# Clustered attention with a routed expert layer: row maxima three steps further ahead, results scaled one head later

## The chip, the cores and the metric

The kernel runs on one core of one Trainium2 chip. A core has five engines that run side by side, each with its own instruction stream: TensorE (PE, matmuls into PSUM; its weight loads are listed as PEld), VectorE (DVE), ScalarE (ACT), GpSimd (POOL) and SyncE (SP, which here only issues DMAs). They wait for each other by semaphores. The metric is the device time of one execution in microseconds (us); lower is better.

## The reference

Two layers are computed. The first is attention for 2 batches x 8 heads, 768 positions, head size 64, in which a query sees only the keys of its own cluster:

```
q_assign = argmax(q_n @ c_n)          # 16 centroids per head
k_assign = argmax(k_n @ c_n)
scores = scale * q @ k.T, or -1e9 where the two assignments differ
attn = softmax(scores);  attn_out = attn @ v
```

The second takes the 1536 tokens (512 numbers each), sends every token to the expert with the largest gate logit (8 experts, at most 384 tokens each), and computes `gate * (relu(x @ w1[e]) @ w2[e])`.

## The kernel before

**Heads and groups.** The 16 (batch, head) pairs are worked off one after the other by a loop over `i`; a head has 12 groups `g` (written below as 6:8, head 6, group 8). Each group issues, in `st_group`, two matmuls of 384 columns for one tile of transposed scores (`s`, L395 and L396; float32 work is done as products of high and low parts) and an exponential on ACT (`pf`, L400). Beside them stands one tile of the row maxima for a later head: `max_tile` issues one matmul (`m`, L335) and one DVE reduction (`mx`, L342). The `m` tiles have two PSUM banks, the `s` tiles three. So in most groups PE issues three matmuls, DVE makes one reduction and ACT one exponential.

**What hangs on the groups** is placed by `hooks(i, g)`, called after each group:

- g = 2 (`G_B1`) and g = 8 (`G_B0`): the two halves of `pv_batch`, 12 matmuls with v into the bank `o` (pool `psO`, one bank). At g = 2 the head before is finished: `p_add` on DVE (`acc`, L406), then `sum_strips` on PE (`rsp`, L432), which sums the exponentials and whose second half reads `acc`; ACT empties both banks (`rs` L443, `oT` L425). At g = 8 stands the `p_add` of the current head's first half.
- g = 5: `sum_turn` (PE transposes `rtp`, L450) and `max_chain`; g = 6: `sum_scale` (DVE, `r`, L456 to L458).
- g = 7: `max_rows` transposes the next head's maxima (`mtp`, L373), ACT copies them (`mr`, L375), SP sends them into row `Qs` of the next head's operand; then `out_stage` (`otp`, L522) turns the result of the head before. `rtp`, `mtp`, `otp` and the cluster tiles `ctb`, `ccp`, `ctp` share the two banks of pool `psT`.
- g = 8: `out_scale` on DVE (`lt`, `lg`, `x`: L543 to L545).
- Even heads assign clusters for the pair of heads two pairs ahead: scores at g = 2, `cl_turn` at g = 4 (`ctp`), the first DVE steps of `cl_assign` at g = 8 (`cmx`, `ceq`), a product on POOL, and the last two (`cm`, `ohb`) at g = 2 of the next head.
- `split` prepares the operands of head i+3: ACT copies at g = 2 and g = 8, each followed by three GpSimd subtractions (`ql`, `Y`, L298) and SP transfers.
- The gate of the first batch (`gate(0)`) begins at 8:9: small DVE steps, matmuls `gps` on PE, and at its end six indirect DMAs on GpSimd that scatter the tokens into the array `xd`. A load of 128 rows of `xd` (`row0`) is issued on SP at 9:6.
- Four `w_split` of expert weights (ACT copy L131, DVE subtraction L137) stand at 12:10, 13:10, 14:4 and 14:10 (`W_AT`).

PE, DVE and ACT keep the written order from head 1 on (`keep`). After the heads, `moe` runs the experts, nearly all of it on PE.

Of the kernel before, what the change touches and what calls it, by code (L numbers as in the profile page):

```python
# [23 lines left out]
def kernel(  # L24
# [655 lines left out]
    def hooks(i, g):  # L680
# [3 lines left out]
        if (i, g) == (H, G_B0 + 1):  # L684
            gens["g"] = gate(0)
        if i == H and g > G_B0 or i == H + 1 and g < 2:
            next(gens["g"], None)
# [3 lines left out]
        if (i, g) in W_AT:  # L691
            c = W_AT.index((i, g))
            w_split(c)
            w_load(c + NA)
# [9 lines left out]
        if g == G_CHAIN and i + 1 < NH:  # L704
            max_chain(i + 1)
        if g == G_ROWS and i + 1 < NH:
            max_rows(i + 1)
        if (i, g) == (H + 1, 4):
# [463 lines left out]
    with ExitStack():  # L1172
        for i in range(NH):
# [3 lines left out]
            for g in range(2 * NT):  # L1177
                st_group(i, g)
                if i == 0 and g < NT:
                    max_tile(1, g, 0, warm=WARM1)  # L1180
                    max_tile(1, g, 1)
                else:
                    n, k = (i + 1, NT + g) if g < NT else (i + 2, g - NT)
                    if n < NH:
                        max_tile(n, k // 2, k % 2)
# [85 lines left out]
```

## Time and profile before

| | us |
|---|---|
| median of 3 runs | 489.12 (489.0 to 489.14) |
| the profiled execution | 489.03 |
| its span from first to last instruction | 486.9 |
| PE busy in it | 449.3 (92%) |
| DVE busy | 319.9 (66%) |
| ACT busy | 273.9 (56%) |
| POOL busy | 128.2 (26%) |
| one reduction `mx` (L342), mean of 192 | 0.552 |

The prologue and head 0 end at 39.2 us, the heads at about 284.4; the experts take the 202.4 us from there to the end of the span. Busy PE time is the union of matmuls whose modelled ends overlap: a matmul of 384 columns is shown with 0.34 us, but in a run of them one starts every 0.18 us. Waits therefore show best as distances between starts. A row of a stretch gives its bounds, its length, the busy us (and instructions) of PE, PEld, DVE, ACT and POOL, the granted TensorE clock as a share of full speed (1.00 is 2.4 GHz, 0.50 is 1.2 GHz), the DMA share and GB/s.

### The profile page before, as it was taken

To read this page: it belongs to the slowest core of one execution; us is meant where nothing else is said; L and a number is where in the kernel's file an instruction comes from. 1 tells how busy PE (TensorE), PEld (TensorE's weight loads), DVE (VectorE), ACT (ScalarE), POOL (GpSimd) and SP (SyncE) were. 2 spreads that over 40 slices of the span, in tenths; PEclk is the share of its full clock that TensorE was granted. 3 is DMA by queue.
4 is the path that set the end of the run, shared out by engine and by line. 5 is a ranking of instruction groups with operands and counts; after the bars stand their busy time and mean duration, and the time that the engine had idled before them with its cause. 6 is when DMAs were issued, how large, how long until landed. Compare 5 with 4: busy or idle time off the path is not lost. (4 is left out here: it accounts for less than half of the span.)

```text
span 486.9 us, 8139 instructions
## 1 busy us (share of the span) xinstructions
PE 449.3 (92%) x2832; PEld 347.0 (71%) x2832; DVE 319.9 (66%) x682; ACT 273.9 (56%) x548; POOL 128.2 (26%) x168
## 2 busy tenths in 40 slices
PE   8899989999999798899888997999999999999984
PEld 8765565656666564666545565699999999999963
DVE  6866767678576872876674365578878787787511
ACT  4744555646456553556445461566868767686530
POOL 6783434452323282232100023000101101010110
PEclk9989999999999997999999999999999999999998
DMA  8368249964332443123211116866887979776110
GB/s 282 87 181 253 84 115 367 320 225 147 92 100 59 120 154 99 49 50 75 67 45 43 44 52 233 290 214 230 268 263 223 276 238 283 257 233 207 36 35 18
DMA packets 31223, 78.14 MB, mean 161 GB/s; under 512 B 4678, under 2 KB 5024, under 8 KB 31172
## 3 DMA queue, kind: packets, MB, share of 16 engines
q1 hardware_dynamic: 26340, 61.33, 42.4%
q0 software_dynamic: 4832, 16.15, 8.6%
q8 instruction: 30, 0.49, 0.4%
q14 instruction: 21, 0.17, 0.1%
HBM read 50.46 MB, written 16.76 MB: 138 GB/s over the span
## 5 line engine op out<-in xcount | busy, mean ns | idle before, releaser
L342 DVE TENSOR_REDUCE mx<-m 128x1 f32<-128x384 f32 x192 | 103.1, 552 | 73.6 <-PE m L335 71.2
L400 ACT ACTIVATE pf<-s 128x384 f32<-128x384 f32 x192 | 90.2, 494 | 70.2 <-PE s L396 68.2
L137 DVE TENSOR_TENSOR ws<-wraw,ws 128x1024 fp32r<-128x1024 f32 x64 | 78.1, 1223 | 29.6 <-ACT ws L131 29.4
L335 PE MATMUL m<-Y,W 112*128 112x384 f32 (+1 forms) x192 | 69.6, 365 | 6.6 <-DVE mx L342 6.3
L395 PE MATMUL s<-W,Y 112*128 112x384 f32 (+1 forms) x192 | 73.4, 382 | 1.7 <-ACT pf L400 1.7
L907 PE MATMUL g<-xc,ws 128*128 128x416 f32 x224 | 70.0, 373 | 1.7 <-DVE yT L916 0.8
L907 PE MATMUL g<-hc,ws 128*128 128x416 f32 x224 | 69.5, 371 | 0.0
L131 ACT ACTIVATE ws<-wraw 128x1024 fp32r<-128x1024 f32 x64 | 67.0, 1050 | 3.7 <-DMA wraw<-in_w_dram 3.6
L396 PE MATMUL s<-Qs,Y 97*128 97x384 f32 (+1 forms) x192 | 66.2, 345 | 2.7 <-DMA row<-xd 2.6
L415 PE MATMUL o<-pf,v 128*64 128x384 f32 x360 | 67.3, 503 | 0.0
L649 POOL DMA_INDIRECT out_dram<-y,row x17 | 18.0, 1057 | 168.2 <-ACT pt L915 85.2
L908 PE MATMUL g<-xc,ws 128*128 128x208 f32 x224 | 58.0, 259 | 0.0
L908 PE MATMUL g<-hc,ws 128*128 128x208 f32 x224 | 57.9, 259 | 0.0
L298 POOL TENSOR_TENSOR Y<-kv,Y 64x256 fp32r<-64x256 f32 x48 | 35.7, 769 | 70.2 <-ACT Y L316 70.1
L395 PEld LDWEIGHTS s<-W,Y 112*128 112x128 f32 (+1 forms) x192 | 36.7, 191 | 21.5 <-issue 17.7
L335 PEld LDWEIGHTS m<-Y,W 112*128 112x128 f32 (+1 forms) x192 | 37.0, 193 | 14.8 <-DVE mx L342 12.2
L298 POOL TENSOR_TENSOR ql<-qv,W 64x256 fp32r<-64x256 f32 x45 | 34.9, 800 | 42.9 <-issue 26.9
L915 ACT ACTIVATE pt<-g 128x208 f32<-128x208 f32 x84 | 27.4, 339 | 31.4 <-PE g L908 27.3
L907 PEld LDWEIGHTS g<-xc,ws 128*128 128x128 f32 x224 | 42.1, 188 | 3.9 <-issue 2.4
L415 PEld LDWEIGHTS o<-pf,v 128*64 128x64 f32 x360 | 23.6, 139 | 29.4 <-issue 29.2
L908 PEld LDWEIGHTS g<-xc,ws 128*128 128x128 f32 x224 | 42.8, 191 | 0.0
L908 PEld LDWEIGHTS g<-hc,ws 128*128 128x128 f32 x224 | 42.8, 191 | 0.0
(206 smaller groups left out, 698.9 us busy)
## 6 DMA issues: line engine op xcount, KB each, us to landing
wraw<-in_w_dram SPq DMA_DIRECT2D x64, 512.0 KB
xd<-z POOLq DMA_DIRECT2D x7, 780.0 KB
row<-xd SPq DMA_DIRECT2D x18, 260.0 KB
qv<-in_qT_dram SPq DMA_DIRECT2D x8, 384.0 KB
kv<-in_kT_dram SPq DMA_DIRECT2D x8, 384.0 KB
v<-in_v_dram SPq DMA_DIRECT2D x8, 384.0 KB
Y<-Y SPq DMA_DIRECT2D x32, 96.0 KB
Qs<-W SPq DMA_DIRECT2D x16, 192.0 KB
```

Source lines behind the costliest of these rows:

```text
L131: keep(nc.scalar.activation(out=w[:, 0], in_=raw[c], func=AF.Copy))
L137: keep(nc.vector.tensor_tensor(out=w[:, 1], in0=t, in1=w[:, 0].bitcast(F32), op=ALU.subtract))
L298: keep(eng.tensor_tensor(out=out[:, cc], in0=a[:, cc], in1=b[:, cc].bitcast(F32), op=ALU.subtract))
L335: keep(nc.tensor.matmul(out=m[:, 0:HALF], lhsT=W[0:KA[h % 2], t * P:(t + 1) * P], rhs=Y1[0:KA[h % 2], j * HALF:(j + 1) * HALF], start=True ...
L342: keep(nc.vector.tensor_reduce(out=mxt[h][:, j, t:t + 1], in_=m[:, 0:HALF], axis=AX.X, op=ALU.max))
L395: keep(nc.tensor.matmul(out=s[:, 0:HALF], lhsT=Y1[0:ka, ks], rhs=W[0:ka, qs], start=True, stop=False))
L396: keep(nc.tensor.matmul(out=s[:, 0:HALF], lhsT=Y0[0:kb, ks], rhs=Qs[0:kb, qs], start=False, stop=True))
L400: keep(nc.scalar.activation(out=pt[h, u][:, slot[0], slot[1]], in_=s[:, 0:HALF], func=AF.Exp, scale=1.0 / float(D) ** 0.5))
L415: keep(nc.tensor.matmul(out=ot[h][j * D:(j + 1) * D, 0:HALF], lhsT=vt[h // 2][:, h % 2, kt, :], rhs=pf[:, n, j], start=(kt == 0), stop=(kt ...
L907: nc.tensor.matmul(out=o, lhsT=w[0], rhs=x.rearrange("p o n -> p (o n)"), start=start, stop=False)
L908: nc.tensor.matmul(out=o[:, 0:RW], lhsT=w[1], rhs=x[:, 0], start=False, stop=stop)
L915: nc.scalar.activation(out=t, in_=o[:, RW:2 * RW], func=AF.Copy)
```

## The change

All of it lies in the heads. (1) The queue of maxima is drawn from one list; in head 0 and at g = 2 of heads 1 to 3 two tiles are taken in a group, so that from head 3 on the last tile of the next head comes at g = 2 in place of g = 5. `max_chain` follows it at once and `max_rows` two groups later. (2) `rtp` moves from `psT` to the bank `o` of `psO`, which is free between g = 2 and g = 8. (3) `out_stage` moves from g = 7 to g = 11 and `out_scale` to g = 2 of the head after, ahead of `p_add`. (4) `cl_turn` and all DVE steps of `cl_assign` move to the next, odd head: `ctp` at g = 1, `cmx` and `ceq` at g = 2, `cm` and `ohb` at g = 8. (5) The gate moves to 9:2, 9:5 and 9:8, `row0` to 10:9. (6) The weight splits move to 13:8, 14:2, 14:8 and 15:2, behind the batches.

```diff
-    G_CHAIN, G_ROWS = 5, 7
-    G_B0, G_B1, G_TURN, G_OUT = 8, 2, 5, 7
+    G_B0, G_B1, G_TURN, G_OUT = 8, 2, 5, 11
+    TWICE = {(0, g) for g in range(6)} | {(1, 2), (2, 2), (3, 2)}
-    W_AT = [(12, 10), (13, 10), (14, 4), (14, 10)]
+    W_AT = [(13, 8), (14, 2), (14, 8), (15, 2)]
...
-        tp = rt_t[h] = psT.tile([P, 512], F32, tag="t", name="rtp")
+        tp = rt_t[h] = psO.tile([P, 512], F32, tag="o", name="rtp")
...
-        if strips_at(i) and g == 4:
-            cl_turn(strips_at(i))
-            gens["c"] = cl_assign(strips_at(i), nc.gpsimd)
+        if i == 1 and g == 4 or not even and 1 < i < NH - 3 and g == 1:
+            p = 2 if i == 1 else (i + 3) // 2
+            cl_turn(p)
+            gens["c"] = cl_assign(p, nc.gpsimd)
...
         if g == G_B1 and i > 0:
             pv_batch(i - 1, 1)
+            if i > 1 and i != H + 2:
+                out_scale(i - 2)
             p_add(i - 1, 1)
             sum_strips(i - 1)
...
             if not even and 1 < i < NH - 3:
-                for _ in gens["c"]:
-                    pass
+                next(gens["c"])
+                next(gens["c"])
+            if i == H + 1:
+                gens["g"] = gate(0)
+                next(gens["g"])
+                next(gens["g"])
...
-            if i > 0 and i != H + 1:
+            if i == H + 2:
+                out_scale(H)
+            if i == NH - 1:
                 out_scale(i - 1)
-            if even and strips_at(i):
-                next(gens["c"])
-                next(gens["c"])
-            if i == 1:
+            if i == H + 1:
+                for _ in gens["g"]:
+                    pass
+            if not even and i < NH - 3:
                 for _ in gens["c"]:
                     pass
...
+                for _ in range(1 + ((i, g) in TWICE)):
+                    if maxima:
+                        n, k = maxima.pop(0)
+                        max_tile(n, k // 2, k % 2, warm=WARM1 if n == 1 and k % 2 == 0 else 0)
+                        if k == 2 * NT - 1:
+                            max_chain(n)
+                            rows_at[2 * NT * i + g + 2] = n
+                if 2 * NT * i + g in rows_at:
+                    max_rows(rows_at[2 * NT * i + g])
```

PE in head 6, from the last score group ahead of `mtp` to the first half of `pv_batch` at 6:8, before the change (words in brackets are the engines or DMA lanes waited for):

```order
L395 MATMUL s_1558<-W01_95,Y101_99 128x384 [waits Activation_49]
L396 MATMUL s_1558<-Qs01_103,Y001_107 128x384
L335 MATMUL m_1562<-Y100_98,W00_94 128x384 [waits DVE_49]
L373 MATMUL mtp_1565<-cs_75,mxx_1538 6x128 [waits DVE_49,PE_49]
L522 MATMUL otp_1570<-rhb_92,oT_1507 128x144 [waits Activation_49]
L522 MATMUL otp_1570<-rhb_92,oT_1507 128x144 x2
L395 MATMUL s_1574<-W01_95,Y101_99 128x384
L396 MATMUL s_1574<-Qs01_103,Y001_107 128x384 [waits Pool_49]
L335 MATMUL m_1578<-Y100_98,W00_94 128x384
L415 MATMUL o_1581<-pf_1445,v_1169 64x384 [waits DMAHW0_49]
L415 MATMUL o_1581<-pf_1445,v_1169 64x384 x5
```

And after it, from `mtp` (now at 6:4) on to the same batch:

```order
L373 MATMUL mtp_1537<-cs_75,mxx_1482 6x128 [waits Activation_49]
L395 MATMUL s_1544<-W01_95,Y101_99 128x384
L396 MATMUL s_1544<-Qs01_103,Y001_107 128x384
L335 MATMUL m_1548<-Y100_98,W00_94 128x384 [waits DVE_49]
L450 MATMUL rtp_1551<-cs_75,rs_1516 128x128 [waits Activation_49]
L450 MATMUL rtp_1551<-cs_75,rs_1516 128x128 x2
L395 MATMUL s_1555<-W01_95,Y101_99 128x384 [waits Activation_49]
L396 MATMUL s_1555<-Qs01_103,Y001_107 128x384
L335 MATMUL m_1560<-Y100_98,W00_94 128x384 [waits DVE_49]
```

and, two groups on:

```order
L395 MATMUL s_1575<-W01_95,Y101_99 128x384 [waits Activation_49]
L396 MATMUL s_1575<-Qs01_103,Y001_107 128x384 [waits Pool_49]
L335 MATMUL m_1579<-Y100_98,W00_94 128x384 [waits DVE_49]
L415 MATMUL o_1582<-pf_1450,v_1186 64x384 [waits DVE_49,PE_49]
L415 MATMUL o_1582<-pf_1450,v_1186 64x384 x5
```

Between `mtp` and the batch stand now four groups and `rtp` in place of `otp`; `mtp` waits for ACT instead of DVE and PE, and the first matmul of the batch carries a wait for DVE, which reads `rtp` out of the bank `o`.

DVE at 6:8 before the change, where the results are scaled (`lt`, `lg`, `x`) and the clusters begun (`cmx`, `ceq`) between two reductions:

```order
L342 TENSOR_REDUCE mx_1549<-m_1578 128x1 [waits PE_49]
L406 TENSOR_TENSOR acc_1588<-pf_1445 128x768 [waits Activation_49]
L543 TENSOR_TENSOR lt_1594<-otp_1570,r_1554 128x48 [waits DVE_49]
L544 TENSOR_TENSOR lg_658<-lg_658,lt_1594 128x48 [waits DVE_49]
L545 TENSOR_TENSOR x_657<-otp_1570,r_1554 128x6x64
L241 TENSOR_REDUCE cmx_1598<-ctp_1527 128x24
L244 TENSOR_TENSOR ceq_1600<-ctp_1527,cmx_1598 128x384 [waits DVE_49]
L342 TENSOR_REDUCE mx_1549<-m_1607 128x1 [waits PE_49]
```

After it, DVE at 7:2, between the last reduction for the next head and the first for the head after that:

```order
L342 TENSOR_REDUCE mx_1526<-m_1652 128x1 [waits PE_49]
L348 TENSOR_TENSOR mxx_1655<-mx_1526 128x6 [waits DVE_49]
L543 TENSOR_TENSOR lt_1663<-otp_1620,r_1564 128x48
L544 TENSOR_TENSOR lg_709<-lg_709,lt_1663 128x48 [waits DVE_49]
L545 TENSOR_TENSOR x_708<-otp_1620,r_1564 128x6x64
L406 TENSOR_TENSOR acc_1667<-pf_1558 128x768 [waits Activation_49]
L241 TENSOR_REDUCE cmx_1684<-ctp_1644 128x24
L244 TENSOR_TENSOR ceq_1686<-ctp_1644,cmx_1684 128x384 [waits DVE_49]
L342 TENSOR_REDUCE mx_1697<-m_1698 128x1 [waits PE_49]
```

The chain of maxima (`mxx`) and the scaling of head 5 now stand ahead of the `p_add` (`acc`) that `rsp` waits for, the clusters behind it.

SP from 9:2 to 9:7 before the change; `mr` carries the row of head 10, `ql` the pieces of head 12, for which GpSimd has its six scatters to issue first:

```order
L308 DMA Qs00_102<-W00_94 64x768 [waits DMAHW6_49,PE_49,Activation_49]
L308 DMA W00_94<-ql_2077 32x768 [waits DMAHW7_49,Pool_49]
L712 DMA row0_2130<-xd_110 128x520 [waits DMASW5_49,DMASW4_49,DMASW6_49,DMASW3_49,DMASW7_49,DMASW2_49,DMAHW0_49,DMASW1_49,DMASW0_49]
L376 DMA Qs01_103<-mr_2146 1x6x128 [waits DMAHW1_49,Activation_49]
L308 DMA Y100_98<-Y100_98 32x768 [waits DMAHW2_49,Activation_49]
```

And after it from 9:2 to 10:4, where `qkm` carries mask rows of clusters and the last `mr` is the row of head 11:

```order
L308 DMA W00_94<-ql_2028 32x768 [waits DMAHW7_49,Pool_49]
L308 DMA Qs00_102<-ql_2028 32x768 [waits DMAHW0_49]
L376 DMA Qs01_103<-mr_2068 1x6x128 [waits DMAHW1_49,Activation_49]
L308 DMA Y100_98<-Y100_98 32x768 [waits DMAHW2_49,Activation_49]
L308 DMA Y000_106<-Y100_98 32x768 [waits DMAHW3_49]
L287 DMA W00_94<-qkm_2216 16x768 [waits DMAHW4_49,Activation_49]
L287 DMA Y100_98<-qkm_2216 16x768 [waits DMAHW5_49]
L287 DMA W10_96<-qkm_2216 16x768 [waits DMAHW6_49,PE_49]
L287 DMA Y110_100<-qkm_2216 16x768 [waits DMAHW7_49]
L308 DMA W10_96<-ql_2261 32x768 [waits DMAHW0_49,Pool_49]
L376 DMA Qs11_105<-mr_2289 1x6x128 [waits DMAHW1_49,Activation_49]
```

The row of head 10 is now issued ahead of the scatters, directly behind the pieces of head 12; the pieces of head 13 (the last `ql` here) come after the scatters, and the row of head 11 stands behind them. `row0` has left this stretch.

## Rows read from the trace of the kernel before

**Rows 1.** Stretches: heads 7, 8 and 9, and a part of head 10.

```profile
134.89:149.23 14.34, 13.90 (x87) 9.12 (x87) 10.81 (x24) 7.64 (x17) 5.04 (x7) 1.00 0.31 86
149.23:167.85 18.62, 16.06 (x113) 10.23 (x113) 12.39 (x30) 10.22 (x20) 5.18 (x7) 1.00 0.39 107
167.85:181.58 13.73, 13.73 (x93) 9.12 (x90) 11.49 (x33) 8.35 (x18) 9.64 (x12) 1.00 0.38 131
...
184.50:190.60 6.10, 6.00 (x22) 3.90 (x24) 3.12 (x6) 3.19 (x5) 1.13 (x2) 0.50 0.36 78
```

**Rows 2.** One row of what PE waited for: total us, times, longest.

```profile
PE otp L522 <- ACT mr L375: 4.4, 11, 0.4
```

**Rows 3.** Timeline of head 6: start, us, engine, instruction, idle before.

```profile
127.47 0.34 PE L335 MATMUL m<-Y,W 112*128 112x384 f32 x1
...
128.29 0.27 PE L373 MATMUL mtp<-cs,mxx 128*6 128x128 f32 x1 [0.49 <-DVE r L457]
...
128.92 1.00 PE L522 MATMUL otp<-rhb,oT 128*128 128x144 f32 x6 [0.36 <-ACT mr L375]
...
134.61 0.44 PE L335 MATMUL m<-Y,W 112*128 112x384 f32 x1 [0.46 <-DVE mx L342]
```

**Rows 4.** Timeline: `mtp` of head 1, and the gate's first matmul in head 8.

```profile
49.71 0.27 PE L373 MATMUL mtp<-cs,mxx 128*6 128x128 f32 x1 [0.95 <-DVE r L456]
...
167.58 0.22 PE L584 MATMUL gps<-goh,trib 128*128 128x96 bf16 x1 [1.27 <-DVE goh L573]
```

**Rows 5.** Timeline of head 10: its row of maxima on SP, and PE.

```profile
181.11 0.51 SPq L308 DMA_DIRECT2D W<-ql  x1
...
182.37 0.75 SPq L376 DMA_DIRECT2D Qs<-mr  x1
...
184.60 0.66 PE L396 MATMUL s<-Qs,Y 97*128 97x384 f32 x1 [2.58 <-DMA row<-xd]
```

**Rows 6.** Timeline: PE behind the weight splits, first and last of four waits.

```profile
236.13 0.45 PE L335 MATMUL m<-Y,W 112*128 112x384 f32 x1 [1.77 <-DVE mx L342]
...
268.10 0.44 PE L395 MATMUL s<-W,Y 128*128 128x384 f32 x1 [0.71 <-ACT pf L400]
```

**Rows 7.** Timeline of the batch at g = 2 in heads 6 and 7.

```profile
120.06 2.16 PE L415 MATMUL o<-pf,v 128*64 128x384 f32 x12
...
120.64 0.95 DVE L406 TENSOR_TENSOR acc<-pf 128x768 f32<-128x768 f32 x1
...
121.81 2.12 POOL L298 TENSOR_TENSOR ql<-qv,W 64x256 fp32r<-64x256 f32 x3 [4.13 <-issue]
...
122.81 0.49 PE L432 MATMUL rsp<-acc,onef 128*32 128x384 f32 x2
...
136.61 2.16 PE L415 MATMUL o<-pf,v 128*64 128x384 f32 x12
...
137.98 2.51 POOL L298 TENSOR_TENSOR ql<-qv,W 64x256 fp32r<-64x256 f32 x3 [2.83 <-ACT W L311]
138.06 0.55 DVE L249 TENSOR_REDUCE cm<-ceq 128x24 bf16<-128x384 bf16 x1
138.64 0.56 DVE L254 TENSOR_TENSOR ohb<-ceq,cm 128x384 bf16<-128x384 bf16 x1
```

**Rows 8.** Timeline: scaling beside GpSimd's subtractions (head 6), and without them (head 14).

```profile
131.75 2.15 POOL L298 TENSOR_TENSOR Y<-kv,Y 64x256 fp32r<-64x256 f32 x3 [7.81 <-ACT Y L316]
...
132.06 0.50 DVE L544 TENSOR_TENSOR lg<-lg,lt 128x48 f32<-128x48 f32 x1
...
262.86 0.21 DVE L543 TENSOR_TENSOR lt<-otp,r 128x48 f32<-128x48 f32 x1
...
263.11 0.21 DVE L544 TENSOR_TENSOR lg<-lg,lt 128x48 f32<-128x48 f32 x1
263.23 0.55 DVE L545 TENSOR_TENSOR x<-otp,r 128x384 f32<-128x384 f32 x1
```

**Rows 9.** Group by line: the copies of the weight splits (busy us, mean ns).

```profile
L131 ACT ACTIVATE ws<-wraw 128x1024 fp32r<-128x1024 f32 x64 | 67.0, 1050 | 3.7 <-DMA wraw<-in_w_dram 3.6
```

More of the change, by code (lines that the diff above doesn't have):

```diff
@@ L683, in hooks @@
             zero_fill(2 * (i - 2) + g // 6)
[L684 to L687, printed above, removed]
         if i == 3 and g == 0:
@@ L690, in hooks @@
                 w_load(c)
[L691 to L694, printed above, removed]
         if i == 0:
@@ L703, in hooks @@
                 split(3, g - 6)
[L704 to L708, printed above, removed]
+        if (i, g) == (H + 1, 11):
             close_tile()
-        if (i, g) == (H + 1, 6):
+        if (i, g) == (H + 2, 9):
             row0.append(wra.tile([P, XR], F32, tag="z", name="row0", bufs=1))
@@ L727, in hooks @@
             sum_scale(i - 1)
-        if (i, g) == (H + 1, 11):
+        if i > 0 and g == (G_B0 - 1 if i == NH - 1 else G_OUT) and i != H + 1:
             out_stage(i - 1)
-        if i > 0 and i != H + 1 and g == G_OUT:
-            out_stage(i - 1)
+        if (i, g) == (H + 2, G_B0 - 1):
+            out_stage(H)
+        if (i, g) == (H + 1, 5):
+            next(gens["g"])
         if g == G_B1 and i > 0:
             pv_batch(i - 1, 1)
+            if i > 1 and i != H + 2:
+                out_scale(i - 2)
             p_add(i - 1, 1)
@@ L740, in hooks @@
                 split(i + 3, 0)
-            if i == H + 2:
-                out_scale(H)
             if not even and 1 < i < NH - 3:
-                for _ in gens["c"]:
-                    pass
+                next(gens["c"])
[3 more added lines that the diff above has]
+                next(gens["g"])
+                next(gens["g"])
             sum_evict(i - 1)
@@ L759, in hooks @@
                 split(i + 3, 2)
-            if i > 0 and i != H + 1:
+            if i == H + 2:
+                out_scale(H)
+            if i == NH - 1:
                 out_scale(i - 1)
-            if even and strips_at(i):
-                next(gens["c"])
-                next(gens["c"])
-            if i == 1:
+            if i == H + 1:
+                for _ in gens["g"]:
+                    pass
+            if not even and i < NH - 3:
                 for _ in gens["c"]:
                     pass
+        if (i, g) in W_AT:
+            c = W_AT.index((i, g))
+            w_split(c)
+            w_load(c + NA)
         if g == G_B0 + 1 and 0 < i < NH - 3:
@@ L1172 @@
     with ExitStack():
+        maxima = [(n, k) for n in range(1, NH) for k in range(2 * NT)]
+        rows_at = {}
         for i in range(NH):
@@ L1178 @@
                 st_group(i, g)
[L1179 to L1185, printed above, removed]
+                for _ in range(1 + ((i, g) in TWICE)):
[7 more added lines that the diff above has]
+                    max_rows(rows_at[2 * NT * i + g])
                 hooks(i, g)
```

## Prediction

> **What bounds the kernel now.** I began with the share of busy time: PE is busy for 92% of the span, but that is a mean over three parts. In the experts PE has work nearly throughout, and the change touches nothing there; what can move is the 245 us of the 16 heads, 39.2 to 284.4. I cut these into stretches, one for each head [rows 1]. Head 9 takes 13.73 us with 13.73 busy, so PE alone fills it; this is what a head costs if nobody waits. Head 7 takes 14.34, head 8 takes 18.62. So every head is a PE head with waits in it, and the question is where each wait sits and who is late. For that I read the list of waits [rows 2] and then the timeline at each gap [rows 3 to 6]. The reader is to see there that PE's waits are short, many, and always behind another engine's queue: DVE for `mtp` and `m`, ACT for `otp`, SP for one row of maxima.
>
> Idle time understates a stall a little. In head 6 `mtp` starts 128.29 − 127.47 = 0.82 us after the `m` before it, where one such matmul follows the next in 0.18; 0.64 is lost, while the row shows 0.49 idle [rows 3]. I add 0.15 to each idle time below.
>
> **What the change removes.**
>
> - *`mtp` behind `r`.* In even heads `ctp` holds one bank of `psT`, so `mtp` has to have the bank of `rtp`, which DVE is still reading. After the change `rtp` lies in `o` and `ctp` in odd heads. 0.64 in heads 2, 4, 6, 8, 10 [rows 3]: 3.2. Head 1 waits 0.95 for the same reason [rows 4]: 1.1.
> - *`otp` behind `mr`.* It follows `mtp` directly and needs ACT's copy first. The list has 11 such waits of 0.4 [rows 2], each with its 0.2 of dead space: head 7 has one and head 9 none, and they differ by 14.34 − 13.73 = 0.61 [rows 1]. Now groups lie between, so 11 × 0.61 = 6.7.
> - *`m` behind the scaling and the clusters.* At the end of even heads DVE has `acc`, `lt`, `lg`, `x`, `cmx`, `ceq` in one piece and `m` waits 0.46 [rows 3]: 5 × 0.61 = 3.1.
> - *The gate's first product* waits 1.27 for DVE [rows 4]; in the new places groups lie between: 1.4.
> - *Row of head 10.* On SP it stands behind `W<-ql` (issued at 181.11) and the load of `xd`, so that it goes out at 182.37 and PE stands 2.58 us for it, until 184.60 [rows 5]. The 6.10 us after that run at a granted clock of 0.50 although PE is busy [rows 1], which costs half of them, 3.05. The row goes out ahead of the scatters now: 2.58 + 0.15 + 3.05 = 5.8.
> - *The weight splits.* Four waits from 1.77 down to 0.71 [rows 6], 5.6 in sum; with 4 × 0.15 it is 6.2. They arise because ACT's copy of 1.05 [rows 9] and a DVE subtraction stand in an ordinary group, where each engine has little room.
>
> Sum: 3.2 + 1.1 + 6.7 + 3.1 + 1.4 + 5.8 + 6.2 = 27.5 us.
>
> **What it adds.** The new cost lies in the two batches of `pv`, where PE has 2.16 us of work and the others little [rows 7].
>
> 1. *`acc` at g = 2.* `rsp` begins to read it 122.81 − 120.06 = 2.75 after the batch starts. Today `acc` starts at +0.58 and takes 0.95 [rows 7]. Ahead of it come now `mxx` (tiny), `lt`, `lg` and `x`, 0.37 from the first to the start of `x` and 0.55 for that [rows 8]: `acc` starts at about +1.6 and ends at +2.55, in time. But in odd heads GpSimd's subtraction starts at +1.37 [rows 7], in pieces of 0.71 to 0.84 (a third of the group), so `acc` may have to let it pass, to +2.1, and end at +3.05: 0.3 late. In even heads GpSimd starts at +1.75, behind `acc`. That they do not run side by side I read from `lg`: 0.50 while a subtraction runs, 0.21 without one, the same instruction [rows 8]. Five odd heads: 1.5. Bounds: 0 if `acc` is not held, 4.2 if it loses a whole piece each time.
> 2. *`cm` and `ohb` at g = 8 of odd heads.* 0.55 and 0.56 of DVE [rows 7] behind `acc`. DVE's work from the start of the batch is then 0.58 + 0.95 + 1.1 = 2.65, and the next reductions (0.55 each) run after it. PE, with two banks for `m`, reaches them at 2.16 + 0.5: 0.3 late in four heads, 1.2. Bounds 0.4 and 3.6 (the 0.9 of both counted against PE).
> 3. *The gate in head 9.* Its DVE work is about 12.39 − 10.81 from head 8 and 11.49 − 10.81 from head 9 [rows 1], 2.3 us, put now into a head whose PE has no slack at 9:5: I take 2.2. Bounds 1 and 3.
> 4. *Doubled maxima at g = 2 of heads 1 to 3.* A second reduction of 0.55 in a group whose `m` takes 0.18 of PE, and `acc` later by 0.55: 0.3 three times, 0.65 and 0.35 more in heads 2 and 3. 1.9; bounds 0.9 and 3.
> 5. *The weight splits at batches.* The 1.05 of ACT [rows 9] is hidden by the 2.16 of the batch at g = 8. At g = 2, ACT also has `rs` and `oT` to empty and the next exponentials to make, with three `s` banks between it and PE; I take 1.2, 1.1 and 0.3: 2.6. Bounds 0 and 6.2, which is what they cost today.
> 6. *Head 1* does its clusters ahead of `sum_scale`, and `pv` at 1:8 needs the bank of `rtp`: 0.8; bounds 0 and 1.6.
> 7. *`o` at g = 8* waits for DVE to have read `rtp`. `r` is made at g = 6, two groups before: about 0.07 in 14 heads, 1.0; bounds 0 and 3.
> 8. *The last head's* turn is two matmuls later, 0.4.
>
> Sum: 11.6. Clusters ready later cost nothing by themselves: their mask rows are issued at the batch at g = 2 and needed by `m` at g = 3 two microseconds later at the earliest; that cover gone, each odd head pays what is missing. The row of head 11 stands behind the pieces of head 13, which wait for the scatters; it is made at 10:4 and needed at 11:0, a margin of some 3 us by my placing of the gate's end.
>
> Net 27.5 − 11.6 = 15.9 from the profiled 489.03: 473.1. The median is 0.09 higher: **473.2**.
>
> On step 1 the Trainium skill (SBUF — State Buffer, section "SBUF: two separate sides") says that VectorE and GpSimd share a port pair by an exclusive lock, and that an operation of VectorE with two SBUF inputs and one of GpSimd shut each other out for the whole instruction, whoever comes first. The two durations of `lg` agree. By that rule `acc` would lose a whole piece wherever GpSimd has started first, and the sum would be that of the first rival below.
>
> **The rivals.**
>
> *GpSimd first everywhere.* If `lt` to `x` stretch beside the subtraction (each as `lg` does, 0.3 more), `acc` misses its place before +1.75 in even heads too and loses 0.75 in each, 0.55 of it on PE's path; odd heads lose a second piece. Nine or so heads at 0.65: +6, 479. For it: `lg` [rows 8]. Against: +1.6 is before +1.75 and the pieces start late in even heads [rows 7].
>
> *The stall of head 10 moves to head 11.* If the gate's end slips so far that the scatters, the pieces of head 13 and the row come over 3 us later than I place them, PE waits at 11:0 as it does at 184.60, clock and all: 473.2 + 5.8 = 479. Against: the gate starts some 9 us later by its place, but the row at stake is due a head later, 14 us.
>
> *Slower.* `acc` is the one wait that takes the place of those removed: if PE runs two `m` tiles ahead of DVE when the batch begins, `acc` starts 0.55 later in the 13 heads that scale ahead of it, and loses a GpSimd piece of 0.84 on top: 13 × 1.39 = 18.1, more than all of the gain; 491.3. It decides once `acc` is late by 1.2 in each head (15.9 / 13), that is, ends at about +4. Against: in heads 6 and 7 `acc` starts at +0.58 [rows 7], so DVE keeps up with PE.
>
> *The costs vanish.* Steps 2, 3, 5 and 7 hide in the batches: 466 to 469.
>
> **How the numbers follow.** Forecast case 0.60, with its own range 469 to 477; GpSimd first 0.17; row of head 11 0.08; costs vanish 0.10; slower 0.03, and 0.02 for smaller losses at many places that leave no change. From the bounds of the sum, all low costs together give 464 and all high ones 485; the range from 466 to 481 holds the forecast, the two middle rivals and most of the last, some 0.85. A change of less than 0.2% (1 us) this measurement can't tell from none. Faster 0.95, same 0.02, slower 0.03.
>
> **What would show it.** Even heads near 13.9 us, odd ones near 14.2; no `otp` among the waits; `mr` of head 10 on SP before its scatters and no clock of 0.50 behind it; no wait of PE above 1 us in heads 12 to 15; `rsp` in odd heads waiting 0.3 for `acc`. It is wrong if `rsp <- acc` adds up to more than 4 us, if PE waits for a row at 11:0, or if ACT's copies at 14:2 and 15:2 stop PE for as long as before.

## The result

The changed kernel takes **470.77 us** (median of 4 runs, 469.93 to 472.46) against 489.06 beside it; the ratio is 0.9631, with a 95% interval from 0.9604 to 0.9658. The forecast was 473.2, its range 466 to 481.

Stretches of the changed kernel's profiled execution (472.46 us, span 470.3): heads 3 to 7, 9 and 10, columns as in [rows 1].

```profile
71.31:86.16 14.85, 14.43 (x94) 9.59 (x92) 12.59 (x27) 8.10 (x17) 9.18 (x12) 1.00 0.99 371
86.16:102.07 15.91, 14.86 (x104) 9.65 (x102) 9.48 (x22) 9.62 (x19) 8.36 (x11) 1.00 0.79 248
102.07:116.20 14.13, 14.11 (x92) 9.35 (x91) 11.89 (x26) 8.09 (x17) 8.81 (x11) 1.00 0.79 266
116.20:130.81 14.61, 14.61 (x103) 9.70 (x102) 9.49 (x22) 9.61 (x19) 5.26 (x6) 1.00 0.33 83
130.81:144.96 14.15, 14.13 (x92) 9.38 (x91) 11.91 (x26) 8.09 (x17) 6.69 (x7) 1.00 0.34 98
...
159.58:176.25 16.67, 14.34 (x96) 8.99 (x95) 14.94 (x40) 8.32 (x18) 7.80 (x9) 1.00 0.32 91
176.25:192.13 15.88, 15.86 (x108) 10.33 (x108) 10.20 (x24) 9.25 (x19) 9.31 (x13) 1.00 0.48 156
```

Heads 6 and 10 of the kernel before, which [rows 1] does not have:

```profile
117.99:134.89 16.90, 15.60 (x105) 10.04 (x104) 10.77 (x24) 10.21 (x20) 4.93 (x7) 1.00 0.33 81
...
181.58:204.31 22.73, 18.86 (x107) 11.81 (x105) 10.80 (x25) 9.86 (x19) 6.78 (x10) 0.85 0.32 83
```

Read the stretches of the changed kernel against these and [rows 1]. Head 6 takes 14.61 us in place of 16.90, and PE is busy in all of it; head 7 takes 14.15 in place of 14.34. Head 10 has neither its long wait nor the clock of 0.50. Three heads still stand out: head 4, by 1.3 against head 6; head 9, which holds the gate now; and head 10, by 1.3 too, which turns two results (12 matmuls of `otp` in place of 6; head 9 has none).

What PE waited for in the changed kernel: total us, times, longest.

```profile
PE m L335 <- DVE mx L342: 3.1, 5, 1.6
...
PE s L395 <- ACT pf L400: 2.0, 4, 0.8
...
PE m L335 <- DMA W<-qkm: 1.1, 1, 1.1
...
PE rtp L450 <- ACT oT L425: 1.0, 1, 1.0
...
PE rsp L432 <- DVE x L545: 0.4, 1, 0.4
PE o L415 <- DVE r L457: 0.4, 1, 0.4
```

No `otp` stands there any more [rows 2], and `m` behind `mx` has fallen to two waits that matter, both in head 9. The places themselves, in the timeline of the changed kernel:

```profile
94.15 0.41 PE L335 MATMUL m<-Y,W 112*128 112x384 f32 x1 [1.05 <-DMA W<-qkm]
...
104.18 2.16 PE L415 MATMUL o<-pf,v 128*64 128x384 f32 x12
...
105.55 2.81 POOL L298 TENSOR_TENSOR ql<-qv,W 64x256 fp32r<-64x256 f32 x3 [2.83 <-ACT W L311]
105.79 1.29 DVE L406 TENSOR_TENSOR acc<-pf 128x768 f32<-128x768 f32 x1
...
107.14 0.52 PE L432 MATMUL rsp<-acc,onef 128*32 128x384 f32 x2
...
119.98 0.95 DVE L406 TENSOR_TENSOR acc<-pf 128x768 f32<-128x768 f32 x1
120.13 1.40 POOL L298 TENSOR_TENSOR ql<-qv,W 64x256 fp32r<-64x256 f32 x1 [4.19 <-issue]
...
123.68 0.27 PE L373 MATMUL mtp<-cs,mxx 128*6 128x128 f32 x1
...
167.39 0.75 SPq L376 DMA_DIRECT2D Qs<-mr  x1
167.85 0.45 PE L335 MATMUL m<-Y,W 128*128 128x384 f32 x1 [0.66 <-DVE mx L342]
168.46 0.21 PE L584 MATMUL gps<-goh,trib 128*128 128x96 bf16 x1
...
175.93 0.44 PE L335 MATMUL m<-Y,W 128*128 128x384 f32 x1 [1.65 <-DVE mx L342]
...
254.17 0.45 PE L395 MATMUL s<-W,Y 128*128 128x384 f32 x1 [0.78 <-ACT pf L400]
```

`mtp` of head 6 (123.68) follows the `m` before it without a wait, where it lost 0.64 [rows 3]. The row of head 10 goes out at 167.39, 8.9 us before that head begins; it was 0.8 us behind its beginning [rows 5]. The gate's product (168.46) has no wait of its own; the gate's DVE work makes `m` wait instead, 0.66 and 1.65. Behind the gate's last steps `cm` and `ohb` also stand on DVE (174.27 to 175.41), so the 1.65 is not the gate's alone.

### The profile page after: what moved, and what is told of

It reads as the page before. It is cut to its first block, busy times and chain, and to the rows that moved or that the text cites. A ratio compares the mean times of both kernels' runs of the same rounds, so it can differ in the third digit from the quotient of the medians.

```text
span 470.3 us, 8149 instructions
## 1 busy us (share of the span) xinstructions
PE 444.9 (95%) x2832; PEld 346.0 (74%) x2832; DVE 321.4 (68%) x682; ACT 272.7 (58%) x548; POOL 138.5 (29%) x168
## 5 line engine op out<-in xcount | busy, mean ns | idle before, releaser
L335 PE MATMUL m<-Y,W 112*128 112x384 f32 (+1 forms) x192 | 68.6, 361 | 5.0 <-DVE mx L342 3.1
L415 PE MATMUL o<-pf,v 128*64 128x384 f32 x360 | 66.2, 496 | 0.4 <-DVE r L457 0.4
L298 POOL TENSOR_TENSOR ql<-qv,W 64x256 fp32r<-64x256 f32 x45 | 39.9, 912 | 51.3 <-ACT W L311 26.2
L298 POOL TENSOR_TENSOR Y<-kv,Y 64x256 fp32r<-64x256 f32 x48 | 41.4, 889 | 43.3 <-ACT Y L316 42.0
```

Of the source, the lines that this page charges most:

```text
L298: keep(eng.tensor_tensor(out=out[:, cc], in0=a[:, cc], in1=b[:, cc].bitcast(F32), op=ALU.subtract))
L335: keep(nc.tensor.matmul(out=m[:, 0:HALF], lhsT=W[0:KA[h % 2], t * P:(t + 1) * P], rhs=Y1[0:KA[h % 2], j * HALF:(j + 1) * HALF], start=True ...
L415: keep(nc.tensor.matmul(out=ot[h][j * D:(j + 1) * D, 0:HALF], lhsT=vt[h // 2][:, h % 2, kt, :], rhs=pf[:, n, j], start=(kt == 0), stop=(kt ...
```

## The experiments

Each experiment's kernel ran in six timed runs beside the kernel before, whose median was 488.3 to 490.2 in these groups; the ratios are to the one beside. The times of one kernel spread over 2.4 to 8.8 us. In the profiled executions what lies ahead of the heads took from 18.7 to 22.7 us and the experts from 202.3 to 205.0, whatever the kernel. The heads repeat to 0.1 us, apart from heads 0 and 1 (next run). So a kernel is read from the lengths of its heads, that is, the distances between the first score matmuls of consecutive heads in its trace (head 15 ends at the experts' first matmul):

| us | 0+1 | 2+3 | 4+5 | 6+7 | 8+9 | 10+11 | 12 to 14 | 15 | sum | median | ratio to before |
|---|---|---|---|---|---|---|---|---|---|---|---|
| before | 36.74 | 31.24 | 31.32 | 31.24 | 32.35 | 37.05 | 47.75 | 18.06 | 265.75 | 489.06 | |
| changed | 36.83 | 30.09 | 30.04 | 28.76 | 31.29 | 30.02 | 40.69 | 18.36 | 246.08 | 470.77 | 0.9631 (0.9604 to 0.9658) |
| r1_changed | 37.10 | 30.10 | 30.13 | 28.77 | 31.33 | 30.03 | 40.70 | 18.36 | 246.52 | 471.26 | 0.9637 (0.9606 to 0.9668) |
| e1_maxima_only | 37.74 | 31.71 | 31.95 | 29.92 | 33.53 | 29.98 | 45.47 | 18.05 | 258.35 | 484.36 | 0.9882 (0.9824 to 0.9940) |
| e5_scaling_only | 38.13 | 29.37 | 30.70 | 29.41 | 32.41 | 34.07 | 44.59 | 17.45 | 256.13 | 477.12 | 0.9785 (0.9737 to 0.9833) |
| e2_splits_back | 36.43 | 30.11 | 30.06 | 28.75 | 31.27 | 29.79 | 44.15 | 17.82 | 248.38 | 473.89 | 0.9690 (0.9642 to 0.9738) |
| e3_turn_back | 37.38 | 30.11 | 30.07 | 28.76 | 31.29 | 29.76 | 40.67 | 17.97 | 246.01 | 472.07 | 0.9654 (0.9612 to 0.9696) |
| e4_scale_behind | 36.41 | 30.56 | 30.59 | 29.45 | 31.23 | 30.45 | 40.69 | 18.36 | 247.74 | 475.36 | 0.9717 (0.9673 to 0.9761) |
| i1_even_own | 36.44 | 29.39 | 30.46 | 28.60 | 30.80 | 30.07 | 40.70 | 18.44 | 244.90 | 470.56 | 0.9613 (0.9577 to 0.9649) |
| p1_copy_later | 40.86 | 29.80 | 30.85 | 28.88 | 31.03 | 29.72 | 40.70 | 18.36 | 250.20 | 475.01 | 0.9740 (0.9705 to 0.9776) |
| g1_gate_back | 36.41 | 29.41 | 30.73 | 28.56 | 32.72 | 29.41 | 40.65 | 18.44 | 246.33 | 472.51 | 0.9659 (0.9618 to 0.9701) |
| i4_all | 36.59 | 29.38 | 28.72 | 28.52 | 31.53 | 31.08 | 41.57 | 17.50 | 244.89 | 469.38 | 0.9597 (0.9566 to 0.9629) |
| i5_best | 37.36 | 29.39 | 28.55 | 28.56 | 31.45 | 29.46 | 44.63 | 17.50 | 246.90 | 471.11 | 0.9657 (0.9615 to 0.9698) |
| i6_own_and_zeros | 36.41 | 29.37 | 28.64 | 28.56 | 30.79 | 29.56 | 40.67 | 18.44 | 242.44 | 467.64 | 0.9547 (0.9502 to 0.9592) |

**r1_changed**, the changed kernel once more.

> The changed kernel once more, on the chip of the other three, as their base. Theory: the heads repeat to 0.1 us each (226.7 us from head 1 to the experts), and what differs between runs of this kernel lies ahead of the heads and in the experts: 470 to 473 us. Rival: the 1.05 us wait for mask rows in head 4 or the clock of 0.50 at the start of head 1 comes and goes, and the heads differ by 1 us or more.

It repeats: every pair of heads lies within 0.1 of the first profile, heads 0 and 1 within 0.3. Its experts took 202.5 us, the first profile's 205.0.

### Where the gain comes from

**e1_maxima_only**: the kernel before with part 1 alone.

```diff
-    G_CHAIN, G_ROWS = 5, 7
+    TWICE = {(0, g) for g in range(6)} | {(1, 2), (2, 2), (3, 2)}
...
+                        if k == 2 * NT - 1:
+                            max_chain(n)
+                            rows_at[2 * NT * i + g + 2] = n
```

> The kernel before with part 1 alone: the maxima from one list, doubled at four heads, chain and rows at once behind them; nothing else moved. Theory (the early maxima carry the gain, since mtp no longer needs the bank of rtp, otp no longer follows mr directly, and the row of head 10 passes SP ahead of the pieces of head 12): 4.3 + 6.7 + 5.8 gone, 1 to 2 added, 474 us (472 to 477), with the waits behind the weight splits (6.2) and the gate (1.4) still there. Rival (the moves of rtp, out_stage and out_scale carry it): above 480 us.

My theory for this run fell: 484.36, on the rival's side; by the sum of its heads it gains 7.4 us. Stretches of heads 6, 7, 9 and 10 of this kernel show where:

```profile
121.17:137.53 16.36, 15.43 (x105) 10.01 (x104) 10.79 (x24) 10.11 (x20) 4.92 (x7) 1.00 0.35 83
137.53:151.09 13.56, 13.56 (x88) 9.13 (x87) 10.82 (x24) 7.61 (x17) 5.25 (x7) 1.00 0.31 92
169.14:184.62 15.48, 15.40 (x94) 10.28 (x90) 12.11 (x33) 8.31 (x18) 11.11 (x14) 0.89 0.40 134
184.62:201.04 16.42, 15.49 (x106) 10.07 (x105) 10.74 (x25) 9.61 (x19) 5.45 (x8) 1.00 0.39 103
```

Odd heads (13.56) lose their whole wait, and head 10 loses its long one: 16.42 in place of 22.73, so the early row alone settles that term, with the gate and the load of `xd` where they were. But in even heads only 0.54 is gained. The timeline of head 6 and of the gate in head 8 of this kernel:

```profile
131.59 0.97 PE L522 MATMUL otp<-rhb,oT 128*128 128x144 f32 x6 [0.48 <-DVE r L457]
...
137.25 0.44 PE L335 MATMUL m<-Y,W 112*128 112x384 f32 x1 [0.45 <-DVE mx L342]
...
168.87 0.22 PE L584 MATMUL gps<-goh,trib 128*128 128x96 bf16 x1 [1.27 <-DVE goh L573]
```

`ctp` still holds one bank of `psT`, so now `otp` has to have the bank of `rtp` and takes over the wait for `r` that `mtp` lost. The wait of `m` at the end of the head, the gate's and those behind the splits stay. After the gate's 1.27 the clock fell (0.89 as the mean of head 9), and head 9 takes 1.9 more than head 7. Head 4 grew by 1.4: `m` waits for mask rows that are due three groups earlier.

**e5_scaling_only**: the kernel before with part 3 alone.

```diff
-    G_B0, G_B1, G_TURN, G_OUT = 8, 2, 5, 7
+    G_B0, G_B1, G_TURN, G_OUT = 8, 2, 5, 11
...
             pv_batch(i - 1, 1)
+            if i > 1 and i not in (H + 1, H + 2):
+                out_scale(i - 2)
             p_add(i - 1, 1)
...
-            if i > 0 and i != H + 1:
+            if i in (H, NH - 1):
                 out_scale(i - 1)
```

> The kernel before with part 3 alone: out_stage at g = 11 and out_scale at g = 2 of the next head (head 8 and the last head as before). Theory: otp no longer follows mr, 0.61 in 9 heads, and m at the end of even heads waits no longer (0.6 in heads 2, 4, 6), while the waits for mtp (0.64), for the row of head 10 (5.8), the gate and the weight splits stay: 7 us less than before, 482 us. Rival (mtp, which itself waits for the bank of rtp, only hands its wait on, and the scaling ahead of p_add makes rsp wait for x in even heads, where the clusters hold a bank): 2 us less or nothing.

The theory holds, and the gain is larger still: 0.9785, by the sum 9.6 us against its 7. A stretch and two lines of the timeline of this kernel:

```profile
117.11:132.71 15.60, 15.12 (x106) 9.99 (x105) 10.62 (x24) 9.74 (x19) 5.60 (x7) 1.00 0.34 83
```

```profile
127.52 0.27 PE L373 MATMUL mtp<-cs,mxx 128*6 128x128 f32 x1 [0.48 <-DVE r L457]
...
182.16 0.41 PE L396 MATMUL s<-Qs,Y 97*128 97x384 f32 x1 [2.81 <-DMA row<-xd]
```

Head 6 loses 1.3: the waits of `otp` and of `m` at its end. `mtp` keeps its wait, and so does head 10, 2.81. The waits behind the weight splits did not stay as they were, though the splits did not move: the first two are 1.05 and 0.92 in place of 1.77 and 1.63. Head 10 gains 2.45, more than head 6: the clock of 0.50 behind its wait lasted some 3 us here and over 6 before. Against that, head 4 has a new wait of 1.09 for its row, and heads 0 and 1 are 1.4 longer. So `m` waited at the end of even heads for scaling and clusters together: taking the scaling away is enough here, and in i1_even_own below, where the scaling is back at g = 8 without the clusters, there is no wait either.

**e3_turn_back**: the changed kernel with `rtp` back in `psT`.

```diff
-        tp = rt_t[h] = psO.tile([P, 512], F32, tag="o", name="rtp")
+        tp = rt_t[h] = psT.tile([P, 512], F32, tag="t", name="rtp")
```

> The changed kernel with rtp back in the pool psT. Theory (the early maxima alone free mtp, which now stands a group ahead of rtp): no wait comes back, 470.8 us within 0.5 either way, pv at g = 8 loses its short wait for DVE. Rival (the prediction's first item: the move of rtp frees mtp): 0.64 in five heads and 1.1 in head 1, 475 us.

The theory holds from head 2 on: no pair differs by more than 0.3. Head 1 alone waits again for `r`, and the last head is 0.4 shorter. So with the maxima early and `otp` at g = 11, the bank of `rtp` no longer matters from head 2 on.

**e2_splits_back**: the changed kernel with the weight splits at their old places.

```diff
-    W_AT = [(13, 8), (14, 2), (14, 8), (15, 2)]
+    W_AT = [(12, 10), (13, 10), (14, 4), (14, 10)]
```

> The changed kernel with the weight splits back at 12:10, 13:10, 14:4 and 14:10. Theory (the batches hide them): the first two cost 1.9 and 1.8 again, the later two about 0.7 each, against 2.1 that the splits at 14:2 and 15:2 cost now: 473.8 us (472.8 to 475). Rival (the waits came from the maxima, which are done by 14:2 anyway): 471 us, within 0.5 of the changed kernel.

473.89, and in heads 12 to 15 it is 2.9 us (61.97 against 59.05): the theory, not the rival. Its sizes were off: the first two waits are 1.03 and 0.90, as in e5_scaling_only, not the 1.77 and 1.63 of the kernel before.

### What the change costs

**e4_scale_behind**: `p_add` ahead of `out_scale` at g = 2.

```diff
-            if i > 1 and i != H + 2:
-                out_scale(i - 2)
             p_add(i - 1, 1)
+            if i > 1 and i != H + 2:
+                out_scale(i - 2)
```

> The changed kernel with p_add ahead of out_scale at g = 2. Theory (acc is late in odd heads, by 0.2 in heads 5, 7, 9, 11 and 0.9 in head 3): all of it comes back, 469.2 us (468.6 to 469.8). Rival (the scaling then delays the next reductions by as much): 470.8 us, with m behind mx at g = 3 in place of rsp behind acc.

Neither: odd heads got longer, 14.83 in place of 14.13, and the sum by 1.2 us against r1_changed. Timeline of the batch at 7:2 of this kernel:

```profile
136.56 2.16 PE L415 MATMUL o<-pf,v 128*64 128x384 f32 x12
...
137.34 0.95 DVE L406 TENSOR_TENSOR acc<-pf 128x768 f32<-128x768 f32 x1
137.93 2.33 POOL L298 TENSOR_TENSOR ql<-qv,W 64x256 fp32r<-64x256 f32 x3 [4.11 <-ACT W L311]
...
138.45 0.50 DVE L544 TENSOR_TENSOR lg<-lg,lt 128x48 f32<-128x48 f32 x1
138.87 0.55 DVE L545 TENSOR_TENSOR x<-otp,r 128x384 f32<-128x384 f32 x1
...
139.56 0.52 PE L432 MATMUL rsp<-acc,onef 128*32 128x384 f32 x2 [0.84 <-DVE x L545]
```

`rsp` waits 0.84 for `x`, although `acc` is ready at 138.29. Both live in `psT`: in odd heads `ctp` holds one bank and `otp` the other until `x` has read it, and `rsp` needs that one. So with `otp` at g = 11 the scaling has to come first there.

**i1_even_own**: no scaling in the batch at g = 2 of odd heads (head 11 apart).

```diff
-        if i > 0 and g == (G_B0 - 1 if i == NH - 1 else G_OUT) and i != H + 1:
+        if i > 0 and g == (G_B0 - 1 if i == NH - 1 or even and i != H + 2 else G_OUT) and i != H + 1:
...
-            if i > 1 and i != H + 2:
+            if i > 1 and even and i != H + 2 or i == H + 3:
                 out_scale(i - 2)
...
-            if i == NH - 1:
+            if i == NH - 1 or even and i > 0 and i != H + 2:
                 out_scale(i - 1)
```

> The changed kernel, but in even heads the result is staged at g = 7 and scaled at g = 8 of the same head, so that the batch at g = 2 of odd heads holds no scaling. Theory (in odd heads rsp waits for x, which frees the bank that it needs, and for acc behind x): the waits of rsp go, 0.2 in heads 5, 7 and 9 and 0.6 in head 3, and even heads stay at 14.6: 1.2 us less than the changed kernel beside it. Rival (the scaling at g = 8 is what made m wait 0.46 in the kernel before, with or without clusters behind it): even heads get 0.4 to 0.6 longer, 1 us more or no change in sum.

The theory: heads 3, 5, 7 and 9 lose 0.76, 0.27, 0.25 and 0.56 against r1_changed, head 6 grows by 0.08. Head 4 gave 0.6 back, for reasons that i4_all takes up. The sum is 1.6 us less, but 0.66 of that lies in heads 0 and 1, which vary. The times beside each other, 470.56 and 471.26, can't tell it.

**p1_copy_later**: in odd heads the copy of q, and so GpSimd's subtractions, after `sum_evict`.

```diff
-            if i + 3 < NH:
+            if i + 3 < NH and even:
                 split(i + 3, 0)
...
             sum_evict(i - 1)
+            if i + 3 < NH and not even:
+                split(i + 3, 0)
             pv_evict(i - 1)
```

> The changed kernel with the copy of q (step 0 of split) behind sum_evict in odd heads, so that GpSimd's subtractions at g = 2 start after acc. Theory (acc is late because GpSimd's subtraction runs beside it): acc takes 0.95 in odd heads in place of 1.29, the wait of rsp behind it goes, heads 5 and 7 take 13.9 in place of 14.13. Rival (acc is late because it stands behind x): acc starts and ends as now, and the wait stays.

Timeline of 7:2 of this kernel:

```profile
137.82 2.16 PE L415 MATMUL o<-pf,v 128*64 128x384 f32 x12
...
139.43 0.95 DVE L406 TENSOR_TENSOR acc<-pf 128x768 f32<-128x768 f32 x1
...
142.80 0.47 ACT L425 ACTIVATE oT<-o 128x384 f32<-128x384 f32 x1
```

On `acc` the theory holds: it starts at the same +1.61, takes 0.95 in place of 1.29, and `rsp` has no wait. The gain is gone all the same (14.26 in head 7): `oT` is emptied later, and `rtp`, which needs its bank, loses 0.17 at g = 5 against i1_even_own. The scores right behind it lose 0.13 more, and 0.06 was lost before the batch: together the 0.38 by which head 7 is longer than in i1_even_own (13.88). The 4 us in heads 0 and 1 come from a wait of 2.7 at the start of head 1, a place that the edit doesn't touch, and a clock of 0.50 for over 6 us around it.

**g1_gate_back**: i1_even_own with the gate at 8:9 to 9:1.

```diff
+        if (i, g) == (H, G_B0 + 1):
+            gens["g"] = gate(0)
+        if i == H and g > G_B0 or i == H + 1 and g < 2:
+            next(gens["g"], None)
...
-            if i == H + 1:
-                gens["g"] = gate(0)
-                next(gens["g"])
-                next(gens["g"])
```

> i1_even_own with the gate back at 8:9 to 9:1 (out of the batches of head 9). Theory (in ordinary groups its product makes PE wait 1.3 and the clock falls behind it, as in e1_maxima_only, where heads 8 and 9 were 1.7 and 1.9 longer than their like): head 8 gets 1.7 and head 9 2.0 against the 2.5 that the gate costs in head 9 now: 1.2 us more than i1_even_own. Rival (without a clock loss the old place is cheaper): 0.5 to 1 us less.

It costs 1.4 us in sum against i1_even_own, near the theory's 1.2, but not where it said: head 8 grows by 1.4, head 9 by 0.5, head 10 is 0.65 shorter, with no fall of the clock; two waits of 1.30 and 1.40 stand in head 9 instead.

### A version that is faster still

**i4_all**: the scaling of i1_even_own, no zero fills in head 4, and the split of 15:2 at 12:8.

```diff
-        if g in (3, 9) and 2 <= i < 6:
-            zero_fill(2 * (i - 2) + g // 6)
+        if g in (3, 9) and i in ZF:
+            zero_fill(2 * ZF.index(i) + g // 6)
...
+    ZF = (2, 3, 5, 7)
-    W_AT = [(13, 8), (14, 2), (14, 8), (15, 2)]
+    W_AT = [(12, 8), (13, 8), (14, 2), (14, 8)]
```

> Three edits to the changed kernel together: the scaling as in i1_even_own; the two zero fills of head 4 and the two of head 5 moved to heads 5 and 7; the weight split of 15:2 moved to 12:8 (places 12:8, 13:8, 14:2, 14:8). Theory: head 4 loses its wait for mask rows, 15.9 to 14.7, since the zeros filled the DMA engines; heads 12 and 13 stay as they are because the batch at g = 8 hides a split, and head 15 gets 0.9 shorter; with i1's 1.2 that is 3.3 us less than the changed kernel beside it. Rival: the mask rows are late by themselves (SP issues them only at 4:2) and head 4 keeps over 1 us of wait; the split at 12:8 costs 0.5 or more, since a Y copy stands on ACT there.

The zeros were it: head 4 takes 14.84 in place of 16.00. But they carried the wait along, to the row of head 8 (first line below), now that head 7 has fills. On the split the rival was right in size: head 12 grows by 0.89 against i1_even_own, as much as head 15 loses. Its reason, the copy of `Y` on ACT, is not shown apart: the scaling of i1_even_own stands on DVE there too. Head 10 is 1.0 longer than in i1_even_own, with a clock of 0.50 in it. Timeline of this kernel:

```profile
143.26 0.41 PE L397 MATMUL s<-Qs,Y 97*128 97x384 f32 x1 [0.45 <-DMA Qs<-mr]
...
216.54 1.06 ACT L132 ACTIVATE ws<-wraw 128x1024 fp32r<-128x1024 f32 x1
...
217.81 1.31 DVE L138 TENSOR_TENSOR ws<-wraw,ws 128x1024 fp32r<-128x1024 f32 x1
...
219.65 0.45 PE L336 MATMUL m<-Y,W 112*128 112x384 f32 x1 [0.67 <-DVE mx L343]
```

**i5_best**: as i4_all, but with the last fills at 5:3, 5:9, 7:3 and 7:4 and the split at 13:2.

```diff
+    ZF = [(2, 3), (2, 9), (3, 3), (3, 9), (5, 3), (5, 9), (7, 3), (7, 4)]
-    W_AT = [(13, 8), (14, 2), (14, 8), (15, 2)]
+    W_AT = [(13, 2), (13, 8), (14, 2), (14, 8)]
```

> The changed kernel with the scaling of i1_even_own, the zero fills of 4:3, 4:9, 5:3 and 5:9 at 5:3, 5:9, 7:3 and 7:4, and the weight splits at 13:2, 13:8, 14:2 and 14:8. Theory: head 4 is 14.8 as in i4_all, and head 8 has no wait for its row, since the last zeros end before 8:0; head 15 is 17.5, and 13:2, which has no copy of an operand on ACT beside it, costs 0.3 at most: the heads from 1 on take 222.5 us, 4 less than in the changed kernel. Rival: head 8 waits again for the row (0.7), or 13:2 costs as much as 12:8 did (0.9): 223.5 to 224.5 us.

Both parts of the rival came true, and the second far beyond it: head 13 takes 17.46 in place of 13.53. Timeline and a stretch of head 13 of this kernel:

```profile
223.20 0.49 ACT L444 ACTIVATE rs<-rsp 128x384 f32<-128x384 f32 x1 [3.29 <-PE rsp L433]
223.59 0.49 ACT L426 ACTIVATE oT<-o 128x384 f32<-128x384 f32 x1
224.10 1.06 ACT L132 ACTIVATE ws<-wraw 128x1024 fp32r<-128x1024 f32 x1
...
225.19 1.23 DVE L138 TENSOR_TENSOR ws<-wraw,ws 128x1024 fp32r<-128x1024 f32 x1 [3.97 <-ACT ws L132]
...
226.94 0.50 PE L336 MATMUL m<-Y,W 128*128 128x384 f32 x1 [2.17 <-DVE mx L343]
```

```profile
227.00:229.00 2.00, 2.00 (x8) 1.97 (x9) 0.90 (x2) 0.20 (x1) 0.00 (x0) 0.55 0.47 116
```

The copy stands on ACT behind `rs` and `oT`, so DVE's subtraction starts at 225.19, after an idle time of 3.97, and every reduction stands behind it; PE stops once both banks of `m` are taken, and then the clock falls. At 14:2 the same order costs 0.4 only; the maxima end there and no reduction follows, which is the likely reason, not one that a run shows by itself.

**i6_own_and_zeros**: i1_even_own with the last four fills at 5:3, 5:9, 6:3 and 7:3.

> The changed kernel with the scaling of i1_even_own and the last four zero fills at 5:3, 5:9, 6:3 and 7:3; the weight splits stay where the change put them. Theory (the wait of head 4 comes from the zeros that fill the DMA engines while its mask rows travel, and one fill at a time is done before the next row): heads 3 to 8 take 14.1, 14.7, 13.9, 14.7, 13.9, 14.7 without a wait for a row, 4 us less than in the changed kernel beside heads 0 and 1, which vary by 1.6 with the clock: 468 us. Rival: the fill in head 6 makes its mask rows or the row of head 7 late and the wait moves there, 0.7 to 1.2: 469 us or more.

Heads 4, 5 and 6 of this kernel:

```profile
88.46:103.24 14.78, 14.78 (x104) 9.79 (x102) 10.03 (x24) 9.14 (x19) 5.24 (x7) 1.00 0.47 130
103.24:117.10 13.86, 13.86 (x90) 9.30 (x90) 11.37 (x24) 8.56 (x18) 8.93 (x12) 1.00 0.81 272
117.10:131.80 14.70, 14.70 (x104) 9.78 (x102) 10.04 (x24) 9.14 (x19) 6.22 (x9) 1.00 0.51 155
```

PE is busy in all of each, and no head waits for a row. 467.64 us, ratio 0.9547; its heads take 4.1 less than r1_changed's (0.7 of it in heads 0 and 1) and 23.3 less than before's.

## Why the prediction was right

The time lies 2.4 us below the forecast. In the heads the change gained 19.7 us (265.75 to 246.08; 19.2 in r1_changed) where the sum had 15.9; the first profile gives 2.6 of that back in the experts and 0.6 ahead of the heads, the second 0.1 and 1.4. That the first profile (472.46) comes within 0.7 of the forecast is luck: its experts and its start took back what the heads gained beyond the sum. Laid out by heads, the sum had 11.8 in heads 2 to 11 and 4.2 in heads 12 to 15; measured are 13.0 and 6.8. Its terms erred both ways:

- **`mtp`, `otp` and `m` at the end of even heads**: right in place. Heads 6 and 7 together gain 2.48. The size of one was off: an odd head that loses its `otp` wait gets 0.78 shorter (13.56 in e1_maxima_only against 14.34), not 0.61; if the even ones gain as much, that is 1.9 over 11 heads. I had taken head 9 as the head without a wait, and it had the gate in it. That `rtp` moves to `o` was named as the cause for `mtp`, and this was wrong but for head 1: e3_turn_back has no such wait from head 2 on without the move, so the early maxima free `mtp`.
- **Row of head 10**: right, and e1_maxima_only shows that the early maxima do it alone. In the changed kernel no row waits at 11:0.
- **Weight splits**: 6.2 was taken off for the old places and 2.6 added for the new ones, 3.6 in net; e2_splits_back measures the move at 2.9. Both terms were too large. At the new places PE loses 0.41 and 0.94 (two waits for `pf`), 1.35. At the old ones a part of the waits came from the scaling ahead of them and goes with it, as e5_scaling_only shows. The reason that I gave, a batch hides them, does not hold at 13:2, where reductions follow, nor at 12:8, where ACT and DVE have more in the batch.
- **`m` of head 14**: the sum did not have that three of its six `m` now stand in heads 1 to 3, which takes some 0.5 (3 × 0.18) out of head 14.
- **`acc` at g = 2**: forecast to end at +3.05 in odd heads and cost 0.3; it ends at 105.79 + 1.29 − 104.18 = +2.90 and costs 0.25 (heads 5 and 7 in i1_even_own), some 1.2 in five heads where the sum had 1.5. In even heads it starts first (119.98, GpSimd at 120.13), takes 0.95, and GpSimd's first piece takes 1.40 in place of 0.73: the first rival asked for the opposite. What I had missed is that `rsp` also waits for `x`.
- **`cm` and `ohb` at g = 8 of odd heads**: 1.2 forecast. In heads 5 and 7 measured nothing: head 7 is 14.15 with 14.13 busy. In head 9 they are a part of the 1.65 below.
- **Gate**: 2.2 forecast; the waits at 9:5 and 9:11 lose 0.66 and 1.65, with the 0.15 each 2.6. The sum had the move at a loss, 1.4 taken off and 2.2 added; g1_gate_back shows that it gains 1.4 beside the other parts.
- **Head 1 and doubled maxima**: 2.7 forecast for both. In head 1 `pv` at 1:8 waits 0.38 for `r`; of the doubled groups only 2:2 has a wait of `m`, 0.12. Heads 2 and 3 are 0.63 and 0.70 longer than heads 6 and 7, where the sum had 0.95 and 0.65; 0.39 of head 3's is `rsp` waiting for `x`. Heads 0 and 1 together are as long as before (36.83, 36.74). Both profiles of the changed kernel have a clock of 0.50 for some 3 us soon after the start of head 1; in five of the other kernels it stands in head 0 instead, as it does before the change, and these take 36.4.
- **Bank `o`**: 1.0 forecast. From head 2 on measured nothing: from 5:7 to 5:9, 6:7 to 6:9 and 7:7 to 7:9 PE takes 3.27 us with `rtp` in `o` and in e3_turn_back alike. **Last head**: 0.4 forecast and 0.4 measured (e3_turn_back).
- **What no step had**: 1.2 in head 4. I named the cover, two us for the mask rows, and what it would cost if it were gone, but did not look for what else the DMA engines do there. i4_all and i6_own_and_zeros show that the zero fills do it.

Two more places of the prediction do not hold. Its sign of even heads near 13.9 us did not come (14.61), and it does not follow from its own sum either, which has 16.90 − 1.86 + 0.07 = 15.1 for head 6. And its high bounds add up to 25.0 us of costs, that is 486.6 us, not 485.

The Trainium skill (SBUF — State Buffer, section "SBUF: two separate sides") lets an operation of VectorE with two SBUF inputs and one of GpSimd shut each other out, the first to start holding the ports. The trace agrees in both directions: `acc` 1.29 behind a subtraction that started 0.24 earlier, and 0.95 where it started 0.15 ahead, with the subtraction stretched to 1.40. In both the delay (0.34 and 0.67) is some 0.14 shorter than what the first had left to run (0.48 and 0.80).

Still open is what makes the experts differ by 2.7 us between runs of the same code. A clock of 0.50 in them is not enough: the changed kernel has one from 292 to 295 us and takes 205.0, i6_own_and_zeros one from 280.5 to 283.5 and takes 202.3. Part 4, the move of the clusters, has no run of its own, and the terms above do not close the sum to better than about 1 us.

## What to carry to other kernels

A wait that moves is not a wait removed: in e1_maxima_only `otp` took over the wait of `mtp`, since the bank, not the order, was short; look for who needs the next bank. A batch on PE hides work of other engines only if their queues are free in time and nothing that PE needs stands behind that work: the same split cost nothing at 13:8, 0.4 at 14:2, 0.9 at 12:8 and 15:2, and 3.9 at 13:2, there with a fall of the clock. When a transfer's slack is cut, list what the DMA engines carry at that time, not only the transfer's own length.

## What the runs showed of the hardware

- The clock after a stall is not settled by the stall's length here. After 2.17 us (i5_best) it was 0.55 in the next two us, after the gate's 1.27 (e1_maxima_only) 0.89 over a head, while after the same 1.27 in the kernel before it stayed at 1.00 in head 9 [rows 1, rows 4]; after the 1.65 in head 9 it stayed at 1.00 in the changed kernel and fell to 0.50 between 176 and 178 us in i4_all.
- While the mask rows of head 4 were issued in the changed kernel, the DMA engines were busy throughout (88 to 92 us, 370 GB/s), and two of these issues on SP took 1.66 and 1.13 us (89.72 and 91.42), where most take 0.5 to 0.7. A long issue is no sign of full engines by itself: one at 119.63 took 1.14 with the engines 0.39 busy.
